# Small attention products on all sixteen 32x32 tiles, and VectorE transpositions of bf16 pairs as 4-byte elements

## The chip, the cores and the metric

The kernel runs on one core of one Trainium2 chip. Its time is the device time of one execution in microseconds (us), the median of several runs. The profile of one execution, taken by the hardware profiler, is read beside it. The engines are named as in the profile: PE is TensorE's matmuls, PEld its weight loads, DVE VectorE, ACT ScalarE, POOL GpSimd, SP SyncE.

## What is computed

The reference is a forward pass and its gradients. The input `x` (2048 rows of 512, bf16) goes through a layer norm; the normed rows go through a recurrent attention and, beside it, through a squared-ReLU MLP, and both are added to `x`. The attention carries eight memory rows from one segment of 32 rows to the next:

```python
for s in range(n_seg):                      # 64 segments of 32 rows
    h = concat([mem, xn[s]])                # 8 memory rows + 32 rows
    q, k, v = (einsum('btd,dhe->bhte', h, W) for W in (Wq, Wk, Wv))  # 32 heads of 128
    p = softmax(where(mask, q k^T * scale, -1e9))
    o = einsum('bhqk,bhke->bhqe', p, v)
    o = einsum('bhte,hed->btd', o, Wo)
    mem = o[:, :8]; outs.append(o[:, 8:])
out = x + concat(outs) + (relu(xn @ w1 + b1)**2 @ w2 + b2)
```

The results are `out` and, for a given gradient of `out`, the gradients of `x`, the first memory, the four attention weights and the MLP's two weights and two biases. The backward pass runs over the segments in reverse, since each segment's memory gradient comes from the one after it.

## The kernel before

**Stages.** The MLP comes first; then 64 forward segments; then a short stage that turns two weight matrices; then 64 backward segments; then the weight gradients, from natural-layout tensors that both segment stages have written to DRAM.

**Layout.** The 32 heads of a segment lie as four groups of eight: partition group `j` (32 partitions, the 32 rows of the segment) and slot `i` (of eight) hold head (i, j). A tensor like q, v or o is 128 partitions x 8 slots x 128 (bf16), so one eviction from PSUM of 128 x 512 is half of it (four slots). The eight memory rows of four segments (a block) are handled together, 32 rows at a time, as the "L" work: L projections, L scores, L products. What a segment does for its own 32 rows is the chain.

**A forward segment** (`chain`, from L909): q, k projected (`proj`, L415), transposed on PE (L312), scores (L931), v projected, softmax on DVE and ACT, transposition of P on DVE (L938, L939), the product o = P v (`diag`, L451), its eviction to `oN` (L316 on DVE, L318 on ACT), its transposition on DVE (`sq_T`, L399, tiles `oN` to `OT`), and the output projection (`wo_part`, L814) whose first rows are the next segment's memory.

**A backward segment** (`chain`, from L1233): gO projected and transposed, dP (L1249), the product d2 = P^T gO, the softmax gradient (L1101 to L1106, four DVE instructions), the small transpositions of dS (L1265 to L1267), the products d1 = dS^T q and d0 = dS k. Each product is a `part`: `diag`, two evictions into `dN2`, `dN1`, `dN0`, two `sq_T` into `dT`, and then 64 matmuls of `dh_part` (L1117, called dh2, dh1, dh0 here) that add up in one PSUM bank (`ps_dRA`) for the gradient of the segment's input rows. Its memory rows go through L1284 (`ps_gm`) to the segment before.

**The product** is 64 small matmuls: 32 rows contracted, up to 32 columns of weights, 128 columns moving. Each term has 32 of them, one per head, and there are two terms (the segment's own rows and the memory rows). `diag` makes it in two halves of 32, each with its own PSUM bank and its own eviction. Head (i, j) runs on the tile of the array at row group j and column group j, so that four tiles, on the diagonal, are used:

```python
bk()[32 * j:32 * j + m, k * P:(k + 1) * P], lhsT=lf(j, i), rhs=rf(j, i),
start=(k == 0 and x == 0), stop=(x == n - 1), tile_position=(32 * j, 32 * j),
```

The L products (`ps_oL`, `ps_dqL`) go through the same function, and L1194 (`own`, in `l_post`) has the same form, followed by matmuls of four rows together (`mm`, L1205) into the same bank.

**The transposition** `sq_T` takes half a tensor (four slots of 128) and turns each 32x32 square on DVE; the squares are made of every fourth column, so that the result can be loaded as weights slot by slot, 128 x 32 at a time.

**What sets the order.** A planner (`_Plan`) simulates the engines with given costs and writes each engine's instructions in that order. The chain's operations have priority 0 and PSUM banks of kind "c"; L work and the MLP weight gradients (L1009) have priority 1 and banks of kind "f" or "m", and fill in. `pe(cost, shape)` gives a cost on PE. Of an operation that may run on DVE or ACT (the evictions, cost `EV_F`), the planner picks the engine. A PSUM tile comes from a pool (`pc`) per operation, so that an operation waits for the bank's former reader; with `NBK` (4, 2, 2) banks of kinds "c", "f" and "m" in the forward stage, and five, one and two of "c", "r" and "f" in the backward stage. DMAs are issued on SP, a few on POOL.

The functions that the change touches:

## Time and profile before

| what | value |
|---|---|
| time, median of 3 runs | 3122.26 us (3120.48 to 3124.76) |
| span of the profiled execution | 3097.7 us |
| median less that span | 24.6 us |
| MLP | 0 to 230 us |
| forward segments | 230 to 1314 us |
| weight turn | 1314 to 1340 us |
| backward segments | 1340 to 2516 us |
| weight gradients | 2516 us to the end |

The page has no time of its own for the profiled execution beyond its span, so the difference to the median of the other runs stands in the table. The stage bounds are read from where the lines of each stage begin. In the profile, "out<-in" names the tiles; a group's row holds its count, its busy time, the mean of one in ns, and the idle time of the engine just before its instructions with what ended it. "issue" as a releaser means that the engine waited for nothing that the profile shows. The waits of an engine are listed as line, releaser, total us, times, longest.

### The profile page before, as it was taken

Reading aid. Unit: us, or ns where it says so; the run is one execution under the profiler, and the core shown is the slowest. Engines: PE = TensorE matmul, PEld = TensorE weight load, DVE = VectorE, ACT = ScalarE, POOL = GpSimd, SP = SyncE. Lnnn points to the kernel's source line nnn. Section 1 sums busy time; section 2 is a strip of 40 time slices with the busy share of each in tenths; the row PEclk is TensorE's granted clock in tenths of the full one; section 3 lists DMA queues with packets and bytes.
Section 4 is the critical chain, followed back from the end, with each engine's and each line's share of the span. In section 5 each row is a group of like instructions: output and inputs, shape, how many; then the busy total and the mean of one; then the engine's idle time right before and its main releaser. Section 6 shows DMA issues by size and latency. Waiting matters only on the chain.

```text
span 3097.7 us, 138545 instructions
## 1 busy us (share of the span) xinstructions
PE 2792.6 (90%) x62681; PEld 1629.5 (53%) x62847; DVE 1538.8 (50%) x3390; ACT 933.7 (30%) x1809; POOL 260.8 (8%) x434
## 2 busy tenths in 40 slices
PE   8998889898889898798888898889899889999999
PEld 6664555555555555564555555555555544444444
DVE  5544545555545455575555565565556521233322
ACT  4323434433434344342233333333333310000000
POOL 1110000000000000100000000000000001121111
PEclk9999999999999999999999999999999989999999
DMA  6647655566665563357677777777777669789861
GB/s 205 217 155 212 173 157 171 160 174 167 163 160 153 162 168 125 98 143 195 184 208 193 204 204 202 207 200 213 208 214 206 201 238 351 223 253 280 253 184 45
DMA packets 554918, 590.54 MB, mean 191 GB/s; under 512 B 250197, under 2 KB 355110, under 8 KB 552150
## 3 DMA queue, kind: packets, MB, share of 16 engines
q1 hardware_dynamic: 538758, 527.06, 59.8%
q0 software_dynamic: 15568, 54.61, 5.3%
q8 instruction: 491, 8.04, 1.2%
q14 instruction: 101, 0.83, 0.1%
HBM read 283.32 MB, written 262.68 MB: 176 GB/s over the span
## 4 chain that ended last, share of the span: by engine, by line
PE 67%; issue 10%; DVE 8%; DMA 8%; SPq 3%; ACT 2%; POOL 1%; ACTq 0%; POOLq 0%; DVEq 0%
PE ps_gw L1448 11%; PE ps_dRA L1117 9%; PE ps_d L451 6%; PE ps_RA L814 4%; PE ps_q L415 4%; PE ps_k L415 3%; PE ps_h L609 3%; PE ps_gO L415 3%; SPq L361 3%; PE ps_dRL L1117 3%; PE ps_v L415 2%; PE ps_dw L1009 2%; PE ps_gm L1284 2%; PE ps_o L451 2%; PE ps_gxb L637 2%
## 5 line engine op out<-in xcount | busy, mean ns | idle before, releaser
L1117 PE MATMUL ps_dRA<-WA,dT 128*32 128x512 bf16 x6144 | 376.6, 385 | 12.9 <-issue 10.4
L1448 PE MATMUL ps_gw<-WA,WB 128*128 128x512 bf16 x1505 | 330.7, 379 | 2.2 <-DVE gwo L316 0.6
L415 PEld LDWEIGHTS <-PA 128*32 128x32 bf16 x8192 | 207.5, 98 | 235.7 <-issue 29.8
L1448 PEld LDWEIGHTS <-WB 128*128 128x128 bf16 x1896 | 185.4, 98 | 225.0 <-issue 1.9
L399 DVE STREAM_TRANSPOSE dT<-dN 128x512 bf16<-128x512 bf16 x384 | 255.5, 692 | 90.7 <-ACT dN L318 89.4
L318 ACT CAST dN<-ps_d 128x512 bf16<-128x512 f32 x356 | 198.8, 588 | 292.0 <-PE ps_d L451 257.2
L1117 PEld LDWEIGHTS <-dT 128*32 128x32 bf16 x6144 | 158.0, 97 | 169.5 <-issue 26.5
L316 DVE CAST gwo<-ps_gw 128x512 bf16<-128x512 f32 x64 | 39.7, 683 | 399.5 <-PE ps_gw L1448 268.2
L814 PE MATMUL ps_RA<-WB,OT 128*32 128x128 bf16 x8192 | 139.3, 223 | 58.2 <-issue 41.9
L318 ACT CAST gwo<-ps_gw 128x512 bf16<-128x512 f32 x64 | 32.9, 599 | 515.3 <-PE ps_gw L1448 357.8
L316 DVE CAST kN<-ps_k 128x512 bf16<-128x512 f32 x117 | 80.9, 691 | 191.4 <-PE ps_k L415 188.4
L415 PE MATMUL ps_q<-WA,PA 128*32 128x512 bf16 x2048 | 160.9, 383 | 9.5 <-DVE PA L951 5.5
L814 PEld LDWEIGHTS <-OT 128*32 128x32 bf16 x8192 | 123.4, 99 | 78.9 <-issue 48.2
L415 PE MATMUL ps_k<-WA,PA 128*32 128x512 bf16 x2048 | 159.7, 380 | 1.6 <-issue 1.3
L451 PEld LDWEIGHTS <-PB 32*32 32x32 bf16 x8192 | 120.4, 93 | 72.6 <-issue 33.9
L415 PE MATMUL ps_gO<-WB,PA 128*32 128x512 bf16 x2048 | 139.5, 418 | 15.1 <-DVE PA L1287 14.9
L1227 POOL COPY bVT<-VR 128x1024 bf16<-128x1024 bf16 x64 | 66.6, 1041 | 959.1 <-PE ps_dP L1249 880.8
L318 ACT CAST qN<-ps_q 128x512 bf16<-128x512 f32 x119 | 69.6, 585 | 197.8 <-PE ps_q L415 194.7
L415 PE MATMUL ps_v<-WA,PA 128*32 128x512 bf16 x2048 | 128.1, 378 | 0.0
L1009 PE MATMUL ps_dw<-sx,anT 128*128 128x512 bf16 x358 | 108.0, 385 | 10.3 <-DMA sx<-in_grad_out_dram 6.6
L399 DVE STREAM_TRANSPOSE OT<-oN 128x512 bf16<-128x512 bf16 x128 | 83.8, 691 | 59.6 <-ACT oN L318 59.0
L1117 PE MATMUL ps_dRL<-WA,LT 128*32 128x512 bf16 x1536 | 111.2, 395 | 1.4 <-issue 1.0
(298 smaller groups left out, 4778.2 us busy)
## 6 DMA issues: line engine op xcount, KB each, us to landing
S_GN<-dN SPq DMA_DIRECT2D x192, 256.0 KB
WA<-S_GN SPq DMA_DIRECT2D x160, 256.0 KB
S_Q<-qN SPq DMA_DIRECT2D x64, 256.0 KB
S_K<-kN SPq DMA_DIRECT2D x64, 256.0 KB
S_V<-vN SPq DMA_DIRECT2D x64, 256.0 KB
S_ON<-oN SPq DMA_DIRECT2D x64, 256.0 KB
bqN<-S_Q SPq DMA_DIRECT2D x64, 256.0 KB
bkN<-S_K SPq DMA_DIRECT2D x64, 256.0 KB
```

What stands on the lines that cost most here:

```text
L316: nc.vector.tensor_copy(out, in_)
L318: nc.scalar.copy(out, in_)
L361: self.plan.add({eng: cost}, lambda e: q.dma_start(out_f(), in_f()), R, W, prio, lat)
L399: self.plan.add({"DVE": 0.70}, lambda e, x=x: nc.vector.transpose(dst[:, x, :, :], src[:, x, :].rearrange("p i (a c) -> p i c a", c=JQ)), ...
L415: nc.tensor.matmul(bk()[32 * j:32 * (j + 1), :], lhsT=win(dc), rhs=Wt(dc, c0), start=(dc == 0), stop=(dc == DC - 1), tile_position=(0, 32 ...
L451: nc.tensor.matmul(bk()[32 * j:32 * j + m, k * P:(k + 1) * P], lhsT=lf(j, i), rhs=rf(j, i), start=(k == 0 and x == 0), stop=(x == n - 1), ...
L609: nc.tensor.matmul(bk()[:, x, :], lhsT=Wt[:, dc, fc * P:(fc + 1) * P], rhs=In[:, dc, :], start=(dc == 0), stop=(dc == DC - 1), skip_group_ ...
L814: nc.tensor.matmul(bk()[32 * jd:32 * (jd + 1), :], lhsT=OTt[:, i, j, :], rhs=Wo[:, JQ * i + j, jd * P:(jd + 1) * P], start=(i == 0 and j = ...
L1009: nc.tensor.matmul(bks[x]()[:], lhsT=anT[x][:, c, :], rhs=sx[z][:], start=(c == 0), stop=(c == TC - 1))
L1117: nc.tensor.matmul(bk()[32 * j:32 * (j + 1), :], lhsT=XT[:, i, j, :], rhs=wtf(t, JQ * i + j), start=(first and i == 0), stop=(last and i = ...
L1227: A({"POOL": 1.0}, lambda e: nc.gpsimd.tensor_copy(VT[:, :, :, M:KA].rearrange("p i j r -> p (i j) r"), VR[:].rearrange("p i j r -> p (i j ...
L1448: nc.tensor.matmul(bks[n]()[:], lhsT=HNc[:, rc, dc * P:(dc + 1) * P], rhs=gns[y][:, hf * 512:(hf + 1) * 512], start=(y == 0), stop=(y == N ...
```

## The change

Three things are done.

1. `diag` puts the 64 matmuls of a product on all sixteen tiles. Row group r of the array holds partition group r of the operands; the head in slot i = 4x + c goes to column group c, so a head's result moves from partition group r to partition group c. Row group r writes its own PSUM bank, two times 128 columns (x = 0, 1) of it. For the chain ("c") a product is one operation of 64 matmuls over four banks; the two evictions (`evict_quad`) take two banks x 256 columns each, and wait for all 64. For L work ("f") it is two operations of two row groups on one pair of banks; the second waits for the first one's eviction. `own` and `mm` in `l_post` likewise. The planner's cost of a product falls from 2 x 0.23 per term to 0.13 per term.
2. `sq_T` transposes pairs of bf16 columns as elements of 4 bytes: 256 elements in place of 512 for each partition, at a planner cost of 0.42 in place of 0.70. The result has the two columns of a pair next to each other, so that the weight loads of `wo_part` and `dh_part` read every second column (`tq`).
3. Heads change their places accordingly (`hs`, `slot4`, `half_of`), which makes the right-hand sides of q, k, v and gO contiguous. In the two segment stages PSUM is one tile `ps` of eight banks (`_View`), so that an operation waits for the readers of the banks that it uses rather than for a pool's release; the bank counter of the backward chain starts at 0 in each segment, and dP's bank is of kind "f" in the first one. The numbers of matmuls, loads and DMAs do not change. Beside this the planner's order of the instructions changes on each engine.

```diff
+    def tq(t, i, k):
+        return t[:, i, :, :].rearrange("p c r -> p (c r)").rearrange("p (u r s) -> p u s r", u=2, s=2)[:, k // 2, k % 2, :]
...
+            if self.ps is not None:
+                return _View(self.ps, ("ps", self.pools[key[0]][0] + key[1]), shape, dt)
...
-                self.plan.add({"DVE": 0.70}, lambda e, x=x: nc.vector.transpose(
-                    dst[:, x, :, :], src[:, x, :].rearrange("p i (a c) -> p i c a", c=JQ)),
+                self.plan.add({"DVE": 0.42}, lambda e, x=x: nc.vector.transpose(
+                    dst[:, x, :, :].rearrange("p i c r -> p (i c r)").bitcast(F32).rearrange("p (i u r) -> p i u r", u=2, r=32),
+                    src[:, x, :].rearrange("p i e -> p (i e)").bitcast(F32).rearrange("p (i a u) -> p i u a", a=32, u=2)),
                     [(sk, half)], [(dk, half)], prio)
...
+        def quad(self, kind):
+            b = self.pools[kind][0]
+            return [(b, b + 1), (b + 2, b + 3)] if kind == "c" else [(b, b + 1)] * 2
+
         def diag(self, kind, nm, terms, rkeys, dst, prio):
             n = len(terms)
-            for half in range(2):
-                bk = self.bank(kind, [P, 512], F32, "ps_" + nm)
-
-                def mm(e, half=half, bk=bk):
-                    for k in range(4):
-                        i = 4 * half + k
-                        for x, (lf, rf, m) in enumerate(terms):
-                            for j in range(JQ):
+            pairs = self.quad(kind)
+
+            def mms(rows):
+                for x in range(2):
+                    for y, (lf, rf, m) in enumerate(terms):
+                        for d in range(JQ):
+                            for r in rows:
+                                c = (r + d) % JQ
+                                i = JQ * x + c
                                 nc.tensor.matmul(
-                                    bk()[32 * j:32 * j + m, k * P:(k + 1) * P], lhsT=lf(j, i), rhs=rf(j, i),
-                                    start=(k == 0 and x == 0), stop=(x == n - 1), tile_position=(32 * j, 32 * j),
-                                    skip_group_check=True,
+                                    self.ps[32 * c:32 * c + m, pairs[r // 2][r % 2], x * P:(x + 1) * P],
+                                    lhsT=lf(r, i), rhs=rf(r, i), start=(x == 0 and y == 0), stop=(y == n - 1),
+                                    tile_position=(32 * r, 32 * c), skip_group_check=True,
                                 )
-                self.plan.add(pe(0.23 * n, "d"), mm, rkeys(half), [bk.key], prio)
-                self.evict(lambda half=half: dst[1][:, 4 * half:4 * half + 4, :].rearrange("p i e -> p (i e)"),
-                           bk, lambda bk=bk: bk()[:], [(dst[0], half)], prio, EV_F)
+            keys = lambda g: [("ps", k) for k in pairs[g]]
+            rk = rkeys(0) + [k for k in rkeys(1) if k not in rkeys(0)]
+            if kind == "c":
+                self.plan.add(pe(0.13 * n, "d"), lambda e: mms(range(JQ)), rk, keys(0) + keys(1), prio)
+            for g in range(2):
+                if kind != "c":
+                    self.plan.add(pe(0.115 * n, "d"), lambda e, g=g: mms((2 * g, 2 * g + 1)), rk, keys(g), prio)
+                self.evict_quad(pairs[g], g, dst, prio)
+
+        def evict_quad(self, pair, g, dst, prio):
+            self.plan.add(EV_F, lambda e: ev(
+                {"DVE": "v", "ACT": "s"}[e], dst[1][:, 4 * g:4 * g + 4, :].rearrange("p (r x) e -> p r (x e)", x=2),
+                self.ps[:, pair[0]:pair[0] + 2, 0:2 * P]), [("ps", k) for k in pair], [(dst[0], g)], prio)
...
+    def slot4(c0):
+        return JQ * (c0 % HW // 512) + c0 // HW
+
+    def hs(s):
+        return JQ * (s % 2) + s // 2
+
     def wf(t):
-        w = Wqkv[t].rearrange("p c (i j e) -> p c i j e", i=NI, j=JQ)
-        return lambda dc, c0: w[:, dc, c0 % HW // P:c0 % HW // P + 4, c0 // HW, :]
+        return lambda dc, c0: Wqkv[t][:, dc, slot4(c0) * JQ * P:(slot4(c0) + 1) * JQ * P]
 
     def wof(dc, c0):
-        i0 = c0 % HW // P
-        return WoT[:, i0:i0 + 4, c0 // HW, dc * P:(dc + 1) * P]
+        return WoT[:, slot4(c0), :, dc * P:(dc + 1) * P]
...
-        sg = Stage(plan, {"c": (pc, NBK[0]), "f": (pc, NBK[1]), "m": (pc, NBK[2])})
+        sg = Stage(plan, {"c": (0, 4), "f": (4, 2), "m": (6, 2)}, pc.tile([P, 8, 512], F32, name="ps"))
...
-                                    bk()[32 * jd:32 * (jd + 1), :], lhsT=OTt[:, i, j, :],
-                                    rhs=Wo[:, JQ * i + j, jd * P:(jd + 1) * P],
+                                    bk()[32 * jd:32 * (jd + 1), :], lhsT=tq(OTt, i, j),
+                                    rhs=Wo[:, JQ * hs(i) + j, jd * P:(jd + 1) * P],
...
-        sg = Stage(plan, {"c": (pc, 5), "r": (pc, 1), "f": (pc, 2)})
+        sg = Stage(plan, {"c": (0, 5), "r": (5, 1), "f": (6, 2)}, pc.tile([P, 8, 512], F32, name="ps"))
...
-                            nc.tensor.matmul(bk()[32 * j:32 * (j + 1), :], lhsT=XT[:, i, j, :],
-                                             rhs=wtf(t, JQ * i + j), start=(first and i == 0),
+                            nc.tensor.matmul(bk()[32 * j:32 * (j + 1), :], lhsT=tq(XT, i, j),
+                                             rhs=wtf(t, JQ * hs(i) + j), start=(first and i == 0),
...
-                bks = [sg.bank("f", [P, 512], F32, "ps_dL") for _ in range(2)]
-                for half in range(2):
-                    def own(e, half=half, ly=ly, lx=lx, bks=bks):
-                        for k in range(4):
-                            i = 4 * half + k
-                            for j in range(JQ):
-                                nc.tensor.matmul(
-                                    bks[half]()[32 * j:32 * (j + 1), k * P:(k + 1) * P], lhsT=q_(ly, j)[:, i, 0:RL],
-                                    rhs=q_(lx, j)[:, i, :], start=(k == 0), stop=False,
-                                    tile_position=(32 * j, 32 * j), skip_group_check=True,
-                                )
-                    A(pe(0.24, "d"), own, lk, [bks[half].key])
-
-                    def mm(e, half=half, bks=bks, xx=xx, yy=yy):
-                        for k in range(4):
-                            i = 4 * half + k
-                            for j in range(JQ):
-                                nc.tensor.matmul(
-                                    bks[half]()[32 * j:32 * (j + 1), k * P:(k + 1) * P],
-                                    lhsT=yy[j][:, i * RL:(i + 1) * RL], rhs=xx[j][:, i * P:(i + 1) * P],
-                                    start=False, stop=True, tile_position=(0, 32 * j), skip_group_check=True,
-                                )
-                    A(pe(0.27, "w"), mm, rk, [bks[half].key])
-                for half in range(2):
-                    sg.evict(lambda half=half: dLN[:, 4 * half:4 * half + 4, :].rearrange("p i e -> p (i e)"), bks[half],
-                             lambda half=half, bks=bks: bks[half]()[:], [("dLN", half)], 1, EV_F)
+                pairs = sg.quad("f")
+                for g in range(2):
+                    bkeys = [("ps", k) for k in pairs[g]]
+
+                    def own(e, g=g, ly=ly, lx=lx, pairs=pairs):
+                        for x in range(2):
+                            for d in range(JQ):
+                                for r in (2 * g, 2 * g + 1):
+                                    c = (r + d) % JQ
+                                    i = JQ * x + c
+                                    nc.tensor.matmul(
+                                        sg.ps[32 * c:32 * (c + 1), pairs[g][r % 2], x * P:(x + 1) * P],
+                                        lhsT=q_(ly, r)[:, i, 0:RL], rhs=q_(lx, r)[:, i, :], start=(x == 0), stop=False,
+                                        tile_position=(32 * r, 32 * c), skip_group_check=True,
+                                    )
+                    A(pe(0.12, "d"), own, lk, bkeys)
+
+                    def mm(e, g=g, pairs=pairs, xx=xx, yy=yy):
+                        for r in (2 * g, 2 * g + 1):
+                            for x in range(2):
+                                for c in range(JQ):
+                                    i = JQ * x + c
+                                    nc.tensor.matmul(
+                                        sg.ps[32 * c:32 * (c + 1), pairs[g][r % 2], x * P:(x + 1) * P],
+                                        lhsT=yy[r][:, i * RL:(i + 1) * RL], rhs=xx[r][:, i * P:(i + 1) * P],
+                                        start=False, stop=True, tile_position=(0, 32 * c), skip_group_check=True,
+                                    )
+                    A(pe(0.27, "w"), mm, rk, bkeys)
+                    sg.evict_quad(pairs[g], g, ("dLN", dLN), 1)
...
+            sg.cnt["c"] = 0
...
-            bk = sg.bank("c", [P, NI, KA], F32, "ps_dP")
+            bk = sg.bank("f" if sg.rings else "c", [P, NI, KA], F32, "ps_dP")
...
+        def half_of(t, x):
+            return t.rearrange("p (r x e) -> p x r e", r=JQ, x=2)[:, x]
...
-                                             rhs=gns[y][:, hf * 512:(hf + 1) * 512],
+                                             rhs=half_of(gns[y], hf),
...
-                        nc.gpsimd.dma_start(out_6[JQ * k + j], wt[:])
+                        nc.gpsimd.dma_start(out_6[JQ * hs(k) + j], wt[:])
```

## Prediction

> **What bounds the kernel now.** I read the page first, then the stages by windows, then pieces of the chain of waits in both attention stages, the groups of the lines that change, and what TensorE waits for. From the page:
>
> ```profile
> PE 2792.6 (90%) x62681; PEld 1629.5 (53%) x62847; DVE 1538.8 (50%) x3390; ACT 933.7 (30%) x1809; POOL 260.8 (8%) x434
> q8 instruction: 491, 8.04, 1.2%
> PE 67%; issue 10%; DVE 8%; DMA 8%; SPq 3%; ACT 2%; POOL 1%; ACTq 0%; POOLq 0%; DVEq 0%
> ```
>
> TensorE carries the chain, and a tenth is "issue", in which it waits for nothing that the profile shows. By stage (the forward and the backward segments; columns: length, then busy PE, PEld, DVE, ACT, POOL, the clock, DMA):
>
> ```profile
> 230.00:1314.00 1084.00, 944.36 (x28283) 580.61 (x28363) 557.61 (x1254) 429.89 (x827) 31.18 (x58) 0.98 0.58 161
> 1340.00:2516.00 1176.00, 1048.07 (x29816) 629.17 (x29816) 683.03 (x1356) 373.53 (x686) 91.23 (x140) 0.96 0.72 198
> ```
>
> A forward segment takes 16.9 us (1084/64), a backward one 18.4, with PE idle for 2.2 and 2.0 us of it. Only these two stages hold changed work. A backward segment after its softmax gradient, in the chain (start, length, what):
>
> ```profile
> 2199.58 1.00 PE ps_d L451 x64
> 2200.58 0.98 PE ps_dRA L1117 x16
> 2201.56 1.00 PE ps_d L451 x64
> 2202.56 3.82 PE ps_dRA L1117 x64
> ```
>
> Product d1, 16 matmuls of dh, product d0, 64 of dh: 6.80 us without a gap, since evictions and transpositions of d1 lie beside PE's work. The forward segment is different, there they are on the path:
>
> ```profile
> 831.74 0.60 PE ps_o L451 x28
> 832.41 0.59 ACT oN L318
> 833.02 1.30 DVE OT L399 x2
> ```
>
> **The product on all tiles.** The timeline of a product (start, length, what):
>
> ```profile
> 1910.82 0.22 PE L451 MATMUL ps_d<-gLN,bPLL 32*8 32x128 bf16 x4
> 1910.88 0.22 PE L451 MATMUL ps_d<-gON,bP 32*32 32x128 bf16 x4
> 1910.93 0.22 PE L451 MATMUL ps_d<-gLN,bPLL 32*8 32x128 bf16 x4
> ```
>
> Four matmuls, on four diagonal tiles, start each 55.5 ns; the 64 of a product take 16 x 55.5 ns = 0.89 us. With sixteen tiles the floor is 4 x 55.5 ns = 0.22. The other bound is what PE takes in when the matmuls are short: product dPL below issues 64 with their loads in 0.52 us (8.1 ns each). It has 32 columns each and bounds the instruction side. I take 0.35, between them, since the loads of some 30 pairs can lie ready. A product saves 0.54 us on PE. The L products and `own` ("f") run in groups of two rows, eight tiles at a time: 0.89 becomes 0.45.
>
> The Trainium skill, "TensorE: Matmul & The Clock Gate", Part 1, says that starts of matmuls never come closer than about 25 ns however few the columns. By it a product would take 64 x 25 ns = 1.6 us, and the kernel would be slower; the 0.52 us of dPL and the 13.9 ns of today's products contradict it on small tiles, and its own Part 3 gives about 4 ns on packed tiles.
>
> **The transposition in 4-byte pairs.** The groups:
>
> ```profile
> L399 DVE STREAM_TRANSPOSE dT<-dN 128x512 bf16<-128x512 bf16 x384 | 255.5, 692 | 90.7 <-ACT dN L318 89.4
> L938 DVE STREAM_TRANSPOSE PB<-P 128x256 bf16<-128x256 bf16 x64 | 28.0, 437 | 0.0
> L939 DVE STREAM_TRANSPOSE PB<-PLp 128x256 bf16<-128x256 bf16 x64 | 25.7, 402 | 0.0
> ```
>
> Half the elements take 402 to 437 ns, so time goes by elements. If a 4-byte element costs what a 2-byte one does: 0.43 against 0.69, over 640 transpositions -166 us of DVE. No 4-byte transposition is in the trace; bounds 0.40 (L939) and 0.69 (no gain), and above that the rival below. I take 0.43, the nearest in elements. Line 399's reads have an 8-byte stride before and after.
>
> Only the first transposition of each product can be on the path. The price on the other side is the weight loads of L814 and L1117, which now read every second column. Loads of 128 columns with an 8-byte stride (from WA, in the weight turn) take 114 ns against 98 dense, so up to 4 ns on 32 columns; the matmuls start no faster (1.79 us for 128 of L814 is 14 ns each, 3.82 us for 64 of L1117 is 60): taken as 0, bound 17,920 loads x 4 ns = 72 us if the cover were gone.
>
> **Forward stage.** Path from the product's start to the first half transposed, before: 0.60 + 0.07 + 0.59 + 0.02 + 0.69 = 1.97 us. After: 0.35 of issue, 0.22 for the last matmul, 0.02, the eviction (ACT 0.59 beside DVE 0.69; DVE has to end its own), 0.02, 0.43 = 1.73. That is -0.24 x 64 = -15. The second half comes at 2.16 (2.66 before), and the first four eighths of L814 cover 0.9 us from 1.73, so nothing waits for it. The 16 L products give 16 x 0.44 = -7 of filler, of which I take half. Against it stands issue. PE's waits:
>
> ```profile
> PE ps_RA L814 <- issue: 41.9, 38, 2.6
> PE ps_RL L814 <- issue: 13.7, 11, 2.6
> ```
>
> 49 times the matmuls behind the product come late. The instruction queue's 491 packets (256 PE instructions each) never start closer than 3.32 us apart, and these idles end 1.2 to 1.6 us after such a packet: PE cannot be fed faster than 256 per 3.3 us. A shorter product ends sooner in the same idle. Half of 0.24 lost in 49 places: +6. Forward: -15 - 4 + 6 = -13 (bounds -22 and 0).
>
> The Trainium skill, "Runtime: NRT & Kernel Launch", Instruction fetch mechanics, has PE's instructions come in blocks of 256 and calls the crossing mostly hidden. By it the +6 would be 0. The 105 us of issue idle in the two stages, in 101 places, do not agree.
>
> **Backward stage.** PE work removed per segment: d2, d1, d0 at 0.54 = 1.62, and dqL and two `own` per four segments, 3 x 0.44 / 4 = 0.33; together 1.95 us, 125 us in 64. This is the lower bound.
>
> The upper one is the path, because the order changes: read from the instruction streams, nearly all segments now run d1, 32 of dh2, 32 of dh1, d0, filler, 32 of dh0. d1 0.35, dh2 1.96 to 2.31, dh1 to 4.27 (its transposition is ready at 0.35 + 0.22 + 0.71 + 0.43 = 1.7), d0 to 4.62, then 1.16 us until eviction and transposition let dh0 start (5.78), the end at 7.74. Against 6.80 that is +0.94 for about 48 segments of the form above; the 16 others had an order like it before and 8.8 us, now -0.9. d2, formerly two halves of 0.5 between the gO evictions and dP, is one of 0.35, up to -0.65. If no filler goes into the 1.16 us: 45 - 14 - 42 = -11. If it is filled, work from elsewhere leaves.
>
> DVE's list changes too. Evictions move from ACT (1675 to 1500 instructions) to DVE (2820 to 3053): 233 x 0.69 = +161 us, which the shorter transpositions pay (-166). One of them stands ahead of d1's transposition; dS's two small transpositions, and so d0, wait behind it. In
>
> ```profile
> PE ps_d L451 <- DVE maskA L1106: 17.9, 26, 2.2
> ```
>
> PE already waits for the softmax gradient; a shorter d2 leaves less to lay over it. I take 0.4 of the 125, -50: more than the path alone, as filler exists (dRL, gL, dw), but most of the freed time meets the DVE chain or the fetch.
>
> **Rest.** Contiguous right-hand sides (q, k, v, gO): 383 ns on L415 and 385 on L1117, strided and dense, so nothing. Weight turn and weight gradients keep their counts: 0. SP and POOL issue the same DMAs; what they carry is only reordered.
>
> **Sum.** Span 3097.7 - 13 - 50 = 3034.7. The median 3122.26 is 24.6 above the span; the page gives no other time for the profiled execution, so I add that: 3059. It is 2.0% below the median; a measurement tells some 0.2% (6.2 us) from no change.
>
> **Rivals.**
> 1. *Fetch takes the gain.* Every product is the same 128 PE instructions (with loads) in less time. For it:
>
> ```profile
> 2217.70 0.88 PE ps_d L451 x53
> 2218.58 1.51 issue
> 2220.09 0.34 PE ps_d L451 x11
> 2224.00 0.52 PE ps_dPL L1151 x64
> ```
>
> a product cut by a late packet, and directly behind it, when instructions are there, a product at full rate. If each of the 49 such idles in the forward and 41 in the backward stage grows by the 0.54 saved: +49, 3108 (3095 to 3120). Against it: 233 packets x 3.32 are only 774 of the 1176 us.
> 2. *dh0 uncovered.* The 1.16 us find no filler: +74, 3133 (3110 to 3140); it turns the forecast from 55 of 64 segments on. Against it: PE is 89% busy with filler at hand.
> 3. *4-byte elements cost as much as two.* At 0.69, +0.26 on the first halves of o, d1 and d0: 3 x 64 x 0.26 = +50, 3109; at 0.90 another +40, 3149. No row excludes it.
> 4. *Rows of tiles do not overlap.* At 0.89, with the eviction now behind all 64 instead of beside the second half: +0.54 on o, d1, d0 and half of d2, 64 x 1.9 = +121, 3180 (slower). Already at 0.62 half of this is back and the gain gone. Against it: the queue is not the limit at 0.52.
> 5. *The clock halves more often.* The records show 32 stretches of 3.4 or 6.8 us at half clock, 20 in the backward stage, each after a window with PE busy under 0.71. One takes 1.7 us or more of work. Should every backward segment without one (44) get one: +75, 3134 (3120 to 3165), slower; it decides from 38 new ones. Against it: mean busy falls from 0.89 only to some 0.85. The Trainium skill's page on TensorE, Part 1, has the clock fall after an idle window of about 3.4 us; this trace drops it in windows that are only half idle.
>
> **Chances.** Forecast (2980 to 3095) 0.60; rivals 0.13, 0.07, 0.07, 0.06, 0.07. Range 2980 to 3135: above it lie the fourth and parts of the third and fifth. Faster than 3116: 0.60 and most of rivals 1 and 3, 0.77; within 0.2%: 0.06; slower: 0.17.
>
> **What the profile after would show.** Matmuls of the product starting some 5 ns apart, 64 in 0.3 to 0.4 us (right), 0.5 or more (wrong); the transposition at 0.40 to 0.45; forward stage about 1071 us, backward 1126; PE's "issue" waits about as often and longer behind products; a new wait of dh0 on dT0. Wrong if the granted clock falls below 0.94 in the backward stage, or issue rises by 50 us.

## The result and the profile after

The changed kernel takes 3121.03 us (median of 20 runs, 3110.33 to 3132.80), the kernel before 3112.49 us in the same series (20 runs, 3098.45 to 3127.63). The ratio is 1.0032, with a 95% interval of 1.0016 to 1.0048: slightly slower, where 2% faster was forecast. The profiled execution of the changed kernel took 3119.83 us at a span of 3118.1, so only 1.7 us lie outside a span. The 24.6 us that the prediction added were therefore mostly the distance of a quick execution of the kernel before (some 3099 us) from the median.

Both operations became faster as they should. From the page and the groups of the changed kernel:

```profile
PE 2748.7 (88%) x62721; PEld 1517.7 (49%) x62847; DVE 1495.3 (48%) x3594; ACT 824.0 (26%) x1605; POOL 259.6 (8%) x434
L424 DVE STREAM_TRANSPOSE dT<-dN 128x256 f32<-128x256 f32 x384 | 156.1, 426 | 55.1 <-ACT dN L338 53.4
L859 PEld LDWEIGHTS <-OT 128*32 128x32 bf16 x8192 | 126.5, 101 | 85.7 <-DVE OT L424 46.5
```

The transposition takes 426 ns in place of 692 (0.43 was forecast). The weight loads that read every second column take 101 ns (from OT, 99 before) and 106 (from dT, 97 before); in the order of the kernel before the same strided loads take 98 and 97, so it is not the stride that lengthens them. A product, in the timeline (start, length, what):

```profile
2025.88 0.28 PE L482 MATMUL ps<-bkN,PB 32*32 32x128 bf16 x16
2025.95 0.27 PE L482 MATMUL ps<-bkLN,PB 32*32 32x128 bf16 x16
2026.13 0.35 PE L482 MATMUL ps<-bkN,PB 32*32 32x128 bf16 x16
2026.27 0.35 PE L482 MATMUL ps<-bkLN,PB 32*32 32x128 bf16 x16
```

From its first matmul to its last end a product takes 0.73 us, where it took 1.07 before (medians of d0). The first 32 matmuls start within 0.12 us, and after a hole of 0.13 us the other 32 start 8.3 ns apart, the last at 0.51 us. That is the pace of the 64 short matmuls of dPL, which was the prediction's upper bound (0.52), and not the 0.35 taken.

By stage (forward and backward; columns as in the prediction):

```profile
229.50:1318.00 1088.50, 935.30 (x28290) 555.26 (x28376) 564.90 (x1333) 391.21 (x750) 30.50 (x58) 0.97 0.56 160
1344.00:2536.00 1192.00, 1007.78 (x29784) 542.74 (x29784) 634.72 (x1484) 301.99 (x558) 91.41 (x140) 0.93 0.72 195
```

In the backward stage PE is 40 us less busy, at a clock of 0.93 in place of 0.96, and yet the stage is longer: 1198 us from its first projection to its last dh matmul, against 1177 in the profile before. What PE waits for there:

```profile
PE ps L482 <- DVE maskA L1151: 63.2, 45, 2.4
PE ps L1162 <- DVE dT L424: 25.8, 28, 1.3
PE ps L482 <- issue: 24.4, 35, 1.8
PE ps L1162 <- issue: 10.6, 13, 2.2
```

The wait of d1 for the softmax gradient grew from 17.9 to 63.2 us, and another has grown beside it: dh0 waits 25.8 us for d0's transposition (2.0 before). In the timeline of one segment (in square brackets the idle time before and what ended it):

```profile
2018.50 0.34 PE L482 MATMUL ps<-bqN,maskA 32*32 32x128 bf16 x16 [1.64 <-DVE maskA L1151]
2019.99 5.96 PE L1162 MATMUL ps<-WA,dT 128*32 128x512 bf16 x64
2027.84 1.91 PE L1162 MATMUL ps<-WA,dT 128*32 128x512 bf16 x32 [1.23 <-DVE dT L424]
```

PE is idle for 1.64 us, then runs d1; the 64 matmuls of dh2 and dh1 take 5.96 us, where 64 of dh took 3.82 in the prediction's example, because the clock is granted at half there; and then 1.23 us of idle before dh0, the 1.16 us that the prediction had worked out.

A table tells where the time of a backward segment went. The tail is the time from d1's first matmul to the end of dh0, the front what lies between that end and the next d1; both are taken from the records of the matmuls, as means over the 64 segments. "At full clock" is the median tail of the segments whose tail holds no stretch at half clock.

| kernel | front, us | tail, us | tail at full clock | tails with half clock |
|---|---|---|---|---|
| before | 10.2 | 8.1 | 7.4 | 6 of 64 |
| before, a second profile | 10.1 | 8.3 | 7.6 | 7 |
| changed | 8.9 | 9.5 | 8.4 | 36 |

The front became 1.3 us shorter per segment, and the tail 1.4 longer: 1.0 of it by the medians at full clock (0.8 by the means there), the rest by the clock. Front and tail together are 18.3 and 18.4 us before and 18.4 after. Whether the shorter front is a gain, or work that has only moved into the tail, is for the runs below to tell.

### The profile page after: what moved, and what is told of

It reads as the page before. It is cut to its first block, busy times and chain, and to the rows that moved or that the text cites. A ratio compares the mean times of both kernels' runs of the same rounds, so it can differ in the third digit from the quotient of the medians.

```text
span 3118.1 us, 138865 instructions
## 1 busy us (share of the span) xinstructions
PE 2748.7 (88%) x62721; PEld 1517.7 (49%) x62847; DVE 1495.3 (48%) x3594; ACT 824.0 (26%) x1605; POOL 259.6 (8%) x434
## 5 line engine op out<-in xcount | busy, mean ns | idle before, releaser
L1162 PE MATMUL ps<-WA,dT 128*32 128x512 bf16 x6144 | 420.9, 425 | 33.7 <-DVE dT L424 25.8
L441 PE MATMUL ps<-WA,PA 128*32 128x512 bf16 x6144 | 371.2, 383 | 13.6 <-DVE PA L996 6.3
L1501 PE MATMUL ps<-WA,WB 128*128 128x512 bf16 x1536 | 332.3, 379 | 0.6 <-DVE gwo L336 0.6
L338 ACT CAST dN<-ps 128x512 bf16<-128x512 f32 x280 | 155.4, 587 | 495.4 <-PE ps L482 418.1
L859 PE MATMUL ps<-WB,OT 128*32 128x128 bf16 x8192 | 145.0, 228 | 57.9 <-issue 31.0
L424 DVE STREAM_TRANSPOSE dT<-dN 128x256 f32<-128x256 f32 x384 | 156.1, 426 | 55.1 <-ACT dN L338 53.4
L441 PE MATMUL ps<-WB,PA 128*32 128x512 bf16 x2048 | 127.9, 392 | 9.7 <-DVE PA L1336 8.7
L1054 PE MATMUL ps<-sx,anT 128*128 128x512 bf16 x358 | 109.3, 394 | 13.9 <-DMA sx<-in_grad_out_dram 8.8
L441 PE MATMUL ps<-WA,PB 128*32 128x512 bf16 x1536 | 107.0, 382 | 1.6 <-issue 1.1
L1505 PE MATMUL ps<-GOc,WA 128*128 128x512 bf16 x486 | 106.9, 379 | 0.5
```

The lines of the kernel that those rows point to most:

```text
L338: nc.scalar.copy(out, in_)
L424: self.plan.add({"DVE": 0.42}, lambda e, x=x: nc.vector.transpose(dst[:, x, :, :].rearrange("p i c r -> p (i c r)").bitcast(F32).rearrange ...
L441: nc.tensor.matmul(bk()[32 * j:32 * (j + 1), :], lhsT=win(dc), rhs=Wt(dc, c0), start=(dc == 0), stop=(dc == DC - 1), tile_position=(0, 32 ...
L859: nc.tensor.matmul(bk()[32 * jd:32 * (jd + 1), :], lhsT=tq(OTt, i, j), rhs=Wo[:, JQ * hs(i) + j, jd * P:(jd + 1) * P], start=(i == 0 and j ...
L1054: nc.tensor.matmul(bks[x]()[:], lhsT=anT[x][:, c, :], rhs=sx[z][:], start=(c == 0), stop=(c == TC - 1))
L1162: nc.tensor.matmul(bk()[32 * j:32 * (j + 1), :], lhsT=tq(XT, i, j), rhs=wtf(t, JQ * hs(i) + j), start=(first and i == 0), stop=(last and i ...
```

## The experiments

Ratios are to the kernel before, run on the same chip in the same series, with 95% intervals.

**One part alone: the transposition.** The kernel before with `sq_T` and the weight loads as changed:

```diff
-                self.plan.add({"DVE": 0.70}, lambda e, x=x: nc.vector.transpose(
+                self.plan.add({"DVE": 0.42}, lambda e, x=x: nc.vector.transpose(
...
-                                    bk()[32 * jd:32 * (jd + 1), :], lhsT=OTt[:, i, j, :],
+                                    bk()[32 * jd:32 * (jd + 1), :], lhsT=tq(OTt, i, j),
...
-                            nc.tensor.matmul(bk()[32 * j:32 * (j + 1), :], lhsT=XT[:, i, j, :],
+                            nc.tensor.matmul(bk()[32 * j:32 * (j + 1), :], lhsT=tq(XT, i, j),
...
```

> The kernel before with the 4-byte transposition and its weight loads alone; the products stay on four diagonal tiles in two halves, heads in their old places. The changed kernel's transpositions took 426 ns against 692. Theory A (order: the new plan costs of the products move d0 behind dh1 and take dh2 out of the softmax gradient's shadow): this kernel is free of that, keeps d0 ahead of dh1, and gains up to 0.27 us at each first transposition on the path, 3 per pair of segments: ratio to the kernel before 0.985 to 0.997. Theory B (the clock: TensorE idles more and is granted half clock more often, 56 stretches against 32): TensorE's load is as before, so the clock stays near 0.977 and the ratio is the same as by A. Theory C (the transposition is off the path and worth nothing): 0.997 to 1.003.

Measured: 1.0162 (1.0140 to 1.0184), 3166.23 us. All three theories missed. The plan took the shorter cost as a reason to reorder: the two halves of d0 came apart 31 times in 64 segments (3 times before), PE's wait on the softmax gradient rose from 17.9 to 59 us and that on `ys` from 9.7 to 39 us, and 20 of 64 tails hold half clock.

**The other part alone: the products.** The changed kernel with the old transposition and its plan cost of 0.70.

> The changed kernel with the old transposition of 2-byte elements (0.69 us, plan cost 0.70), all sixteen tiles kept. Theory A: the order d1, dh2, dh1, d0, dh0 comes with the products, so this kernel has the whole loss and none of the transposition's gain: ratio to before 1.01 to 1.03, waits of the product on the softmax gradient around 60 us as in the changed kernel. Theory B: the same direction, granted clock at or below 0.957. Theory C (each half worth nothing): 1.000 to 1.006.

Measured: 1.0309 (1.0287 to 1.0332), 3208.59 us. Beyond the expected range: front 10.2, tail 9.5 us, that is, the slow tail of the changed kernel without its short front. Each half alone is slower than both together, so the halves can't be added up: each of these kernels comes with an order of its own.

**The transposition with the order held.** As the first run, but with the plan's cost left at 0.70, so that no instruction changes its place:

```diff
-                self.plan.add({"DVE": 0.42}, lambda e, x=x: nc.vector.transpose(
+                self.plan.add({"DVE": 0.70}, lambda e, x=x: nc.vector.transpose(
```

> As the run with the 4-byte transposition alone, but with the plan's old cost of 0.70 for it, so that every engine's order is that of the kernel before to the instruction. What is left is the transposition's own worth. If the order made the run with the pairs alone 1.6% slower (theory O), this one is as fast as the kernel before or faster: ratio 0.984 to 0.998, stage times at most those of before. If the 4-byte transposition or the strided weight loads themselves cost time (theory S), it stays slow: 1.010 to 1.018.

Measured: 0.9979 (0.9962 to 0.9997), 3107.81 us. The operation is worth 0.2%, some 6 us; its weight loads cost nothing that shows. The 1.8% between this run and the first come from one number in the plan. This is also the one run whose interval lies below the kernel before.

**The clock.** The changed kernel with seven matmuls more per segment in the softmax gradient's wait:

```diff
+WARM = 7
...
+            def warm(e):
+                for x in range(WARM):
+                    nc.tensor.matmul(sg.ps[:, x % 4, :], lhsT=ident[:], rhs=gN[:, 0:4, :].rearrange("p i e -> p (i e)"),
+                                     start=True, stop=True)
+            A(pe(0.216 * WARM, "f"), warm, [bk.key, ("gN", 0)], [("ps", x) for x in range(4)], 0)
             smax_bwd("A", bk, KA, Pt[z], ("Pt", z), dS, "dS", 0, 0.51)
```

> The changed kernel with seven matmuls of 128x128x512 (1.5 us) more in each backward segment, into the PSUM banks that product d1 overwrites, behind dP and d2 and ahead of d1, so that TensorE is busy while DVE works on the softmax gradient; their result is not used. Theory B: half-clock stretches of the backward stage fall from 38 (174 us) to under 20, its mean clock from 0.93 to 0.96 or more, and the stage is 30 to 50 us shorter than in the changed kernel: ratio to before 0.985 to 0.995. Theory A: the clock may rise but the stage is set by the order of d0 and by DVE: within 10 us of the changed kernel, or slower by what of the 1.5 us is not covered: ratio 1.00 to 1.015.

Measured: 1.0040 (1.0015 to 1.0064), 3126.82 us. The backward stage, at a clock of 0.98:

```profile
1340.50:2532.50 1192.00, 1053.84 (x30103) 561.39 (x30095) 667.80 (x1549) 261.97 (x480) 91.05 (x140) 0.98 0.73 195
```

The stretches at half clock in this stage fell from 38 to 8, tails with half clock from 36 to 7, and the tail from 9.5 to 8.4 us. But the front rose from 8.9 to 10.1: the added matmuls take 1.5 us where the idle was 1.0 us on average, they wait 27.0 us in all for the evictions of d2, whose banks they use, and the plan moved 73 instructions from ACT to DVE on their account. So half clock does lengthen the tail, and this way of avoiding it costs the front what the tail gains. What the clock alone is worth this run can't tell: theory B's forecast is missed, but its cause is not refuted.

**The order.** The changed kernel with d0 raised by 1.5 in the plan's rank:

```diff
+LIFT = (1.5, 0.0, 0.0)
...
-                self.plan.add(pe(0.13 * n, "d"), lambda e: mms(range(JQ)), rk, keys(0) + keys(1), prio)
+                self.plan.add(pe(0.13 * n, "d"), lambda e: mms(range(JQ)), rk, keys(0) + keys(1), prio, lift=lift)
...
-                sg.diag("c", "d%d" % t, terms, rk, ("dN%d" % t, dN[t]), 0)
+                sg.diag("c", "d%d" % t, terms, rk, ("dN%d" % t, dN[t]), 0, LIFT[t])
```

> The changed kernel with one number: the rank of product d0 in the plan is raised by 1.5, so that the plan puts it ahead of dh1 in all segments (d1, 16 of dh2, d0, 16 of dh2, dh1, dh0), the order of the kernel before. Theory A: the wait of dh0 on its transposition (25.8 us in the changed kernel) falls under 5 and d0's eviction lies beside dh1: 0.6 to 1.2 us per backward segment, ratio to before 0.978 to 0.992. Theory B: the idle time in the softmax gradient stays, clock stays about 0.957, and with it the time: ratio 0.998 to 1.006. Theory C (fetch takes what the order gives): issue idles of TensorE rise by 30 us or more, ratio 0.998 to 1.005.

Measured: 1.0041 (1.0026 to 1.0056), 3126.26 us. The ratio fits B and C. The clock stayed at 0.957, as B had it, but the wait did not stay, and the issue idles speak for C. PE's waits in its backward stage:

```profile
PE ps L483 <- issue: 64.7, 49, 3.4
PE ps L483 <- DVE maskA L1152: 39.6, 39, 2.5
PE ps L1163 <- issue: 29.1, 32, 3.0
```

The wait of dh0 on its transposition is gone, and the one on the softmax gradient fell to 39.6. In their place the issue idles went from 41 to 96 us: products d1 and d0, 256 instructions with their loads, now stand within some 2 us of each other.

**What PE instructions cost.** The changed kernel with 64 very short matmuls per segment in the same wait, and, for the base, with one at the same plan cost:

```diff
+            def pad(e):
+                for x in range(64):
+                    nc.tensor.matmul(sg.ps[32 * (x % 4):32 * (x % 4) + 32, x // 16, 0:8], lhsT=gN[:, 0, 0:32], rhs=ident[:, 0:8],
+                                     start=True, stop=True, tile_position=(0, 32 * (x % 4)), skip_group_check=True)
+            A(pe(0.5, "f"), pad, [bk.key, ("gN", 0)], [("ps", x) for x in range(4)], 0)
```

> The changed kernel with 64 matmuls of 32 columns of weights and 8 columns moving in each backward segment, behind d2 and dP and ahead of d1, in the time in which TensorE waits for the softmax gradient: 128 PE instructions and about 0.5 us of PE more per segment. Theory F (TensorE gets 256 instructions in no less than about 3.3 us wherever they are dense): issue idles of the backward stage rise from 41 us by 40 or more, the time by 40 to 100 us against the run with one such matmul. Without F: the pad lies in an idle of 1.4 us, at most 20 us longer.

> The same plan and order as the run with 64 small matmuls, but one matmul in their place: the base of that comparison. Against the changed kernel it differs only by a slightly different order of the filler: within 0.6% of it either way (ratio to before 0.998 to 1.010).

Measured: 3244.95 us (ratio 1.0425, 1.0395 to 1.0456) with 64, 3134.20 us (1.0062, 1.0043 to 1.0081) with one. The order of all other work is the same, so 63 matmuls and their loads cost 110.75 us, 1.73 us per segment. In the timeline of one segment the 64 together take 0.87 us. PE's waits in the backward stage with 64, and then with one:

```profile
PE ps L482 <- issue: 81.4, 46, 3.9
PE ps L1315 <- issue: 47.1, 26, 3.7
PE ps L1162 <- issue: 30.4, 21, 4.1
```

```profile
PE ps L482 <- issue: 34.1, 31, 2.7
PE ps L482 <- DVE maskA L1151: 31.9, 45, 1.6
PE ps L1162 <- issue: 24.2, 23, 3.3
```

These issue idles rise by 101 us (line 1315 is the added matmuls). They end, as in the kernel before, 1.4 us (median) after a packet of the instruction queue has landed, and packets start 3.3 us apart or more. 126 instructions are 126/256 of a packet, 1.6 us at that rate: about what was measured. So theory F is borne out in kind, and the time is just above its range (40 to 100 us): what is dense in PE instructions is paid near the rate of the packets, even beside a wait that PE has anyway (31.9 us in the base). Not all of the 1.73 us need be the packets': the stage's time at half clock rose as well, from 157 to 242 us by the clock records.

**A product of the old length.** First a try that went row group by row group:

```diff
-                        for d in range(JQ):
-                            for r in rows:
+                        for r in rows:
+                            for d in range(JQ):
```

> The changed kernel, order and plan unchanged, but the 64 matmuls of a product issued one row group after the other, so that only four tiles run together and the product takes 0.9 us again in place of 0.41. If the tiles' speed is worth what the prediction's steps say (0.5 us on o, d1 and d0 in each segment, 64 x 1.5 = 96 us), the ratio to before is 1.02 to 1.035. If instruction fetch sets the pace of the products and what lies behind them (theory F), a slower product only takes the place of issue idles: ratio 1.003 to 1.015, with TensorE's issue idles of both stages falling from 98 us to under 70.

Measured: 1.0063 (1.0039 to 1.0088), 3132.02 us. The edit did not do what it was meant to: in its timeline the second half of a product begins at 0.26 us as before, for sixteen matmuls in a row still go to sixteen different tiles. It tells nothing on theory F; it is nearly a second sample of the changed kernel, with the same front (8.9 us) and a tail of 9.7. The next one let each four tiles take their four matmuls in turn:

```diff
-                for x in range(2):
-                    for y, (lf, rf, m) in enumerate(terms):
-                        for d in range(JQ):
+                for d in range(JQ):
+                    for x in range(2):
+                        for y, (lf, rf, m) in enumerate(terms):
```

> The changed kernel, plan and order unchanged, with the 64 matmuls of a product issued so that each four tiles take their four matmuls before the next four tiles begin: the product should take 0.9 us again in place of 0.41 (matmuls about 13.5 ns apart). Unlike the run that went row by row, whose matmuls stayed 6.3 ns apart. If the product's length is on the path as the prediction's steps have it, three times 0.5 us per backward and once per forward segment: up to 64 x 1.5 + 64 x 0.5 = 128 us longer than the changed kernel, ratio to before 1.02 to 1.045. If the order, DVE and instruction fetch set the path (theory F): under 40 us longer, ratio 1.005 to 1.017.

Measured: 1.0042 (1.0024 to 1.0060), 3113.97 us. A product's matmuls now start over 0.65 us, not over the expected 0.85, but 0.14 us longer than in the changed kernel, whose 0.51 the two expectations had put at 0.41. The kernel is no slower (1.0032 and, in the second sample, 1.0063). Tails with half clock fall from 36 to 21, issue idles of both stages from 98 to 81 us. So between 0.51 and 0.65 us a product's length is worth nothing here on balance, with the fewer half-clock tails that came along with the longer one.

**The old transposition in the new order.** The changed kernel with the operation of before at the plan cost 0.42:

> The changed kernel, plan and order unchanged, with the old transposition of 512 elements (0.69 us) and the dense weight loads. In the kernel before's order the transposition was worth 0.2%. In this order, in which dh0 waits for d0's transposition and d1's eviction, d1's and d0's transpositions are on DVE ahead of it: 0.27 us on o, d1 and d0, 64 x 0.8 = 50 us longer than the changed kernel, ratio 1.012 to 1.025. If it is as little as in the other order: 1.004 to 1.009.

Measured: 1.0079 (1.0051 to 1.0106), 3125.25 us. Against 1.0032 and 1.0063 the transposition is worth 0.2 to 0.5% in this order as well, less than the path's arithmetic had it.

**The order alone.** Both of these together, so that the plan, the layout and the PSUM use are the changed kernel's and the operations are nearly the old ones (the evictions still wait for a whole product, which belongs to the change):

> The changed kernel's plan, order, PSUM use and layout, with the product stretched (four tiles in turn) and the old transposition: what is left of the change is nearly the order alone. Theory O (the order carries the loss: d0 behind dh1, dh2 not in the softmax gradient's shadow): ratio to before 1.007 to 1.014, backward segments at full clock 17.7 us or more against 17.1 before. If the loss were in the clock and the fetch that dense products bring: 1.000 to 1.004.

Measured: 1.0061 (1.0041 to 1.0081), 3126.37 us; the median is just under the expected range, its tail at full clock 8.95 us, its front 8.8, and tails with half clock 21. The backward stage, and the same two waits in it:

```profile
1340.50:2544.00 1203.50, 1016.71 (x29829) 561.38 (x29826) 753.80 (x1484) 302.73 (x559) 91.66 (x140) 0.96 0.72 194
PE ps L481 <- DVE maskA L1150: 63.7, 48, 2.2
PE ps L1161 <- DVE dT L424: 35.8, 45, 1.5
```

So the loss is there without the faster operations, and with hardly more half clock (22 stretches in the stage against 20): the stage is 27 us longer than before at the same mean clock of 0.96. The short front is there as well: the 1.3 us are the order's, and no gain of the operations. On top of this order the faster operations give back between nothing and 0.3% (1.0063 and 1.0032), with the stage at 0.93. What this run holds together, the order, the layout and the evictions behind a whole product, was not separated further.

**The order mended.** d2's first half transposed within the softmax gradient, d2 evicted on ACT alone, d0 raised by 1, so that PE runs 16 of dh2 ahead of d1 as in the kernel before:

```diff
+LIFT = (1, 0.0, 0.0)
+TLIFT = ((0.0, 0.0), (0.0, 0.0), (2, 0.0))
...
-                self.evict_quad(pairs[g], g, dst, prio)
+                self.evict_quad(pairs[g], g, dst, prio, {"ACT": 0.59} if dst[0] == "dN2" else EV_F)
...
```

> The changed kernel with three settings of the plan: d2's first half is transposed on DVE within the softmax gradient (rank raised by 2), d2 is evicted on ACT alone, and d0 is put ahead of dh1 (rank raised by 1). TensorE's order becomes d2, 16 of dh2, d1, 16 of dh2, d0, dh1, dh0, that of the kernel before, and the bursts of small matmuls stand further apart than in the run with d0 early. Theory F (dense small matmuls run out of instructions, the order has to spread them): the wait on the softmax gradient falls from 63 us to under 30, issue idles of the backward stage stay below 60, half clock below 30 stretches: ratio to before 0.985 to 0.998. If DVE is the bound of the path: the 0.43 us that delay the softmax gradient cost 27 us, and the ratio is 1.000 to 1.012.

Measured: 0.9997 (0.9973 to 1.0021), 3103.11 us, between the two expectations. The tail is 8.2 us (7.3 at full clock), as before the change, and the front 10.0, also as before. PE's waits in its backward stage:

```profile
PE ps L1164 <- DVE dT L426: 51.1, 47, 1.5
PE ps L484 <- issue: 45.3, 40, 3.5
PE ps L484 <- DVE maskA L1153: 16.8, 22, 1.4
```

The wait on the softmax gradient fell to 16.8 us, but dh2, which now stands in its place, waits 51.1 us for its own transposition, and the issue idles rose to 74. Tails with half clock are 32. The two runs with the stretched product in mended orders:

> The run with d0 early, with the product stretched to four tiles in turn. Theory F (dense products next to each other run out of instructions): issue idles of the backward stage fall from 96 us to under 70 and the time falls by 10 us or more although each product is 0.25 us longer: ratio 0.996 to 1.002. Without F the longer products add up to 64 x 2 x 0.25 = 32 us: 1.006 to 1.014.

> The run with d2's transposition early, with the product stretched to four tiles in turn. Theory F: issue idles of the backward stage fall from 74 us to about 55, half clock from 34 to some 25 stretches, ratio 0.993 to 0.999. Without F: 1.002 to 1.010.

Measured: with d0 early 1.0047 (1.0028 to 1.0065), with d2 early 0.9996 (0.9977 to 1.0014). The issue idles of the backward stage fell from 96 to 84 and from 74 to 70 us, less than expected, and the times stayed where they were: neither better, as F had it, nor worse by the longer product. Half clock in tails fell from 32 to 25 and from 32 to 14. F as an account of these two orders is not confirmed; that a product's length within this range is worth nothing is.

**A shorter warm-up.** Four added matmuls in place of seven:

> As the run with seven extra matmuls in the softmax gradient's wait, with four (0.86 us), and the plan's order that comes with it: 32 of dh2 ahead of d1, d0 right behind d1 or ahead of dh1. Clock theory with cover: the stretches at half clock fall as with seven (9 in the backward stage against 38), without the 0.64 us that did not fit: ratio to before 0.985 to 0.998. Theory F: d1 and d0 next to each other are 256 instructions within 1.3 us, and issue idles take back what the order gives, as with d0 early: 0.998 to 1.008, issue idles in the backward stage over 70 us.

Measured: 1.0105 (1.0074 to 1.0135), slower than either theory had it. The plan put all of dh2 ahead of d1; the tail is the shortest of all (7.4 us) and the front the longest (11.4), as d1 now waits for work that had been in the tail.

**A second profile of the kernel before.**

> The kernel before, unchanged, for a second profile: forward stage within 10 us of 1081, backward within 15 us of 1177, half clock 20 to 30 stretches in the backward stage, if one profile is typical of the kernel.

Measured: forward 1095 us (14 above the first, more than expected), backward 1181.5, half clock in 20 stretches of the backward stage; span 3116.6. One profiled execution's stages are good to some 15 us, no better.

## Why the prediction was wrong

- **Backward stage, -50 us: the step that failed.** The changed kernel has 1198 us against 1177 and 1181.5, and its near copy, the row-by-row run, has 1211: about +25. The prediction took 0.4 of the 125 us of freed PE work as gain, "more than the path alone, as filler exists". The freed time became idle time and half clock instead: by the two stage rows PE is 40 us less busy and idle for 184 us in place of 128, and the clock is 0.93 in place of 0.96. Filler was not what ran short. The 16 matmuls of dh2 (0.98 us) that the kernel before ran in 45 of 64 segments in the softmax gradient's shadow moved into the tail, and PE sat idle in the shadow (63.2 us of wait against 17.9). The prediction saw this order in the instruction streams and listed dh2 wholly behind d1, without asking what had filled the wait before. Its -0.65 us for d2 is of the same kind: d2 lay beside the softmax gradient already. It had +0.94 us on the stretch from d1 to dh0, against 1.0 measured at full clock; that is in part luck, since it took 0.35 us for each product where 0.51 was measured, and an uncovered dh0 in some 48 segments where it waits in 28.
- **The product's saving.** 0.35 us was taken, 0.51 measured between first and last start: the saving is 0.38, not 0.54, and the three products of a backward segment free 1.14 us, not 1.62. The choice between the bounds was wrong, since the nearer row (64 pairs in 0.52 us) was the answer. Why the first half of a product goes faster than the second the runs don't show.
- **The transposition**: 0.43 forecast, 0.426 measured; on the weight loads nothing, as forecast. But of the some 170 us that it saves on DVE the evictions took most: 204 instructions moved from ACT to DVE by the pages (the prediction had 233 more on DVE and 175 fewer on ACT, which don't agree), and DVE is only 43.5 us less busy.
- **Forward stage, -13 us.** Eight profiles with this forward order and both fast operations have 1067 to 1084 us, mean 1076; the kernel before has 1081 and 1095, mean 1088. The number came as forecast, but not by the forecast's path, so it is luck. From the product's start to the first half transposed, the medians are 2.12 us before and 2.05 after, -0.07 and not -0.24. And five profiles with the same forward order and a slower product or transposition have 1071 to 1082, mean 1077: in the order alone that path takes 2.53 us and the stage 1081. The 12 us, if they are more than scatter, go with the order and the PSUM use.
- **The clock** (rival 5) did come, at a chance of 0.07, and the prediction's own sign of being wrong with it: a clock below 0.94 in the backward stage, 0.93 measured. Half-clock stretches went from 20 to 38 in the backward stage, and with the idle now right ahead of the tail they fall on the tail: 36 of 64 against 6. The price per segment was put at one stretch on 44 more segments; 30 more tails had one, and the mean tail rose some 0.4 to 0.6 us beyond what it did at full clock. Half clock is not needed for a loss, as the order alone shows. But by the table the front's 1.3 us outweigh the tail's 1.0 at full clock, so whether the changed kernel would still be slower at the clock of before is open: no run takes the half clock away without adding work.
- **Fetch** (rival 1) is real, with a price of up to 1.73 us for 63 matmuls with loads. In the changed kernel itself the issue idles hardly moved (105 to 98 us); where the order is mended they come back (96 and 74 us in the backward stage).
- **Rivals 2, 3 and 4**: the idle before dh0 is there in 28 segments (25.8 us), so rival 2 had the right place and less than half the price; 3 and 4 are refuted by the two operations' own rows.

What stays open: why the sum of front and tail, 18.2 to 18.6 us, hardly moves between all the orders tried with both fast operations and without added matmuls, and is the 18.3 and 18.4 of the kernel before, while its parts move by 1.5 us. The mended order does not get the short front as well because 16 of dh2 are in the front again and wait there for their transposition (51.1 us). That DVE's list is the common bound was not tried, nor were the products on sixteen tiles with the order of before.

The Trainium skill, "Runtime: NRT & Kernel Launch", Instruction fetch mechanics, calls the crossing of a block of 256 instructions mostly hidden. For PE in this kernel it is not: 126 more instructions cost 1.73 us.

## What to carry to other kernels

When a planner orders the work, a cheaper operation is also a new plan: hold the order fixed (leave the planned cost as it was) to see what the operation itself is worth, and only then let the plan move; here that was 0.2% faster against 1.6% slower for the same operation. Before counting freed engine time as gain, ask what used to lie in the waits and whether it still does: work that moves out of a wait lengthens the path that it moves onto. Bursts of small matmuls are paid by instruction as well as by length, and a wait left open ahead of a dense stretch can be paid again as half clock in that stretch.

## What was not expected of the hardware

- 64 matmuls on sixteen tiles with a load each start 3.3 ns apart for the first half, stop for 0.13 us, and then go at 8.3 ns each.
- 63 matmuls with loads, in a stretch where PE otherwise idles, cost 1.73 us, twice the 0.87 us that they take; a part of it may be half clock.
- The clock fell to half mostly behind waits of 1 to 2 us: with the added matmuls in that wait the backward stage had 8 such stretches, without them 38.
